# A top-k attention and expert kernel: the chain of a score tile cut from 14 steps to 12

## The chip, the cores and the metric

The kernel runs on one core of a Trainium2 chip. The metric is the device time of one execution in microseconds (us); the time of a kernel is the median of its runs, and lower is better.

## The reference

Three layers follow each other. `q`, `k` and `v` are 4 x 8 x 576 x 64 in float32, the token matrix after attention is 2304 x 512.

```python
scores = q @ k.T / sqrt(64)                       # per batch and head, 576 x 576
kth    = 32nd largest score of each row
attn   = softmax(where(scores >= kth, scores, -1e9))
x      = attn @ v                                 # 2304 x 512
h      = max(x @ w1, x @ w2, x @ w3);  x = h @ w_out      # 512 -> 768 -> 512
e      = argmax(x @ w_gate); gate = softmax weight of e     # 8 experts
out    = gate * (relu(x @ ew1[e]) @ ew2[e])       # 512 -> 1024 -> 512
```

## The kernel before, in words

**Tiles.** The scores are worked through in 144 tiles of 128 rows by 576 columns (36 for each of the 4 batches). Four tiles that follow each other make a group (`G = 4`), and some quantities, the threshold above all, are computed once for a group.

**Steps.** The order of all work is written out by hand. One loop (lines 1585 to 1735) counts steps `t`; in each step it issues, for tiles of different age, the stages below, and each engine works off its own queue in that order. A stage of tile `n` stands in step `n + L`, and the constants `L_...` (lines 612 to 618) are the ages. In the kernel before: ScalarE evicts the scores of tile `t + 1` (`st_evac`); VectorE takes the eight largest of each of six chunks (`st_chunks`, age 0) and merges them in a chain of small instructions (`st_rounds`, the step after); ScalarE marks the scores above the 24th (`st_over`, age 2); GpSimd takes those out (`st_rest`, 3); VectorE takes the next eight (`st_next8`, 4). After the fourth tile of a group VectorE finds the 32nd value of all four (`st_pick` at the end of one step, `st_kth` in the next, age `L_KTH` = 8 for the group's first tile).

**Behind the threshold.** Two tiles of each group are masked by VectorE: ScalarE takes the exponent (`st_exp`, age `L_MASK` = 9, first thing in the step) and VectorE multiplies it by the comparison with the threshold (`st_mask`, same step, at the end of VectorE's list `bulk`). The other two, for which `early(n)` is true, are masked before the exponent: ScalarE makes a mark (`st_gap`, age 7 or `L_MASK - 2`), GpSimd subtracts it from the scores (`st_drop`, a step later), and ScalarE's exponent comes in the middle of its step (age 9). Then for each tile ScalarE writes the upper 16-bit half of the result (`st_split`, age 10, last of ScalarE's big instructions in the step), GpSimd subtracts it to get the lower half (`st_split2`, 11), a DMA transposes both (`st_ptr`, 12), and TensorE multiplies with `v` (`st_av`, 14).

**What runs beside it.** The `bulk` list is worked off by `run_bulk`, and after each of its entries `micro` issues one instruction of every open chain, so that chains of small dependent VectorE instructions lie between larger ones. `st_kth` is such a chain of two instructions (lines 998 and 999), `st_rounds` one of five. `finish` issues what is left of a chain at the end of the step. The dense layers and the experts are cut into units, small batches of matmuls; `run_units` issues them behind the attention matmuls of a step, as a credit that grows by a fixed amount per step allows (1.08, later 1.4 and 1.8). Weights of the dense layers are split into halves in the first steps (`prep_w`, list `wq`): two pieces a step while `t < L_KTH - 2` = 6, then one.

**Buffers.** The exponents have `NE3` = 3 buffers, the split pairs `NPH` = 3, the score tiles `L_MASK + 2` = 11.

**Behind the last tile.** The loop goes on after step 144 until the last tiles have passed the chain; `finale` then works through the rest of the experts.

Of the kernel before, what the change touches and what calls it, by code (L numbers as in the profile page):

```python
# [19 lines left out]
def kernel(  # L20
# [61 lines left out]
    G = 4  # L82
# [12 lines left out]
    def attempt(ctx, general):  # L95
# [518 lines left out]
        L_REST = L_OVER + 1  # L614
        L_N8 = L_REST + 1
        L_KTH = L_N8 + G - 1 + 1
        L_EXP, L_MASK = L_KTH, L_KTH + 1
        L_SPLIT, L_LO, L_PTR, L_AV = L_MASK + 1, L_MASK + 2, L_MASK + 3, L_MASK + 5
        LAG = L_AV + 2
        NE3 = L_LO - L_MASK + 1  # L620

        with ExitStack() as p1:
            p_wt = p1.enter_context(ExitStack())
# [12 lines left out]
            wst, m_ps = [p_w.enter_context(tc.tile_pool(name="wst", bufs=6, side="right"))], []  # L636
# [34 lines left out]
            def after(n, fn):  # L671
                due.setdefault(clock[0] + n, []).append(fn)

            def chain(fns):
                chains.append(list(fns))
                return chains[-1]

            def micro():
                for c in list(chains):
                    if c:  # L680
                        fn = c.pop(0)
                        if fn is not None:
                            fn()
                    if not c:
                        chains.remove(c)

            def finish(c):
                while c:
                    fn = c.pop(0)
                    if fn is not None:  # L690
                        fn()
# [3 lines left out]
            def run_bulk():  # L695
                bulk.extend(tail_bulk)
                tail_bulk.clear()
                while bulk:
                    bulk.pop(0)()
                    micro()  # L700
# [46 lines left out]
            def split_tile():  # L747
                if clock[0] < 0:

                    tag = ("e", NE3) if lead_n[0] < NE3 else ("f", NFB)  # L750
                    lead_n[0] += 1
# [229 lines left out]
            def st_kth(g):  # L981
                kt = sm_p.tile([P, G], F32, tag="kth", name="kth") if general else hkth[:, g]
                kth[g] = kt
                if general:
                    m8 = sm_p.tile([P, 8], F32, tag="m8", name="m8")

                    def search(i):
                        wfall = wk_p.tile([P, S], F32, tag="f", name="f", bufs=NFB)
                        src = Ss[g * G + i]
                        for rnd in range(TOP // 8):  # L990
                            nc.vector.max(out=m8, in_=src)
                            if rnd < TOP // 8 - 1:
                                nc.vector.match_replace(out=wfall, in_to_replace=m8, in_values=src, imm_value=LOW)
                                src = wfall
                        nc.vector.tensor_copy(out=kt[:, i:i + 1], in_=m8[:, 7:8])
                    return chain([lambda i=i: search(i) for i in range(G)])
                return chain([
                    lambda: nc.vector.tensor_tensor(out=y8[g], in0=hsel[:, g % NHS], in1=y8[g], op=ALU.mult),
                    lambda: nc.vector.tensor_reduce(out=kt, in_=y8[g], axis=AX.X, op=ALU.add),
                ])  # L1000
# [19 lines left out]
                after(4, total)  # L1020


            def early(n):
                return n % G >= G - (ZN[n // G % len(ZN)])

            def st_gap(n):
                g, i = divmod(n, G)
                zz[n] = wk_p.tile([P, S], U16, tag="g", name="g", bufs=NGB)
                nc.scalar.activation(out=zz[n], in_=Ss[n], func=ACTF.Sign, scale=-1.0, bias=kth[g][:, i:i + 1])  # L1029

# [3 lines left out]
            def st_exp(n):  # L1034
                g, i = divmod(n, G)
                e = wk_p.tile([P, S], F32, tag="e", name="e", bufs=NE3)
                ee[n] = e
                nc.scalar.activation(out=e, in_=Ss.pop(n) if early(n) else Ss[n], func=ACTF.Exp, scale=ESC, bias=be[g][:, i])  # L1038

            def st_mask(n):  # L1040
                g, i = divmod(n, G)
                e = ee[n]
                nc.vector.scalar_tensor_tensor(out=e, in0=Ss.pop(n), scalar=kth[g][:, i:i + 1], in1=e,  # L1043
                                               op0=ALU.is_ge, op1=ALU.mult)

            def st_split(n):
                p = ee[n]
                ph = phl[n % NPH]
                nc.scalar.activation(out=ph[:, 0, 0:S], in_=p, func=ACTF.Copy)  # L1049
# [242 lines left out]
            def piece_ok(i):  # L1292

                if i >= KE:
                    return bool(e2) and i < KE + 2 * KD
                return bool(picked) and clock[0] > picked + 8 and clock[0] > FREE + (0 if i < KE // 2 else L_AV + 1)

            def piece(i):

                st = stage()  # L1300
                re = nc.sync.value_load(firsti[0:1, 0:1], min_val=0, max_val=NE - 1)
                if i < KE:
                    src = ew2[bass.ds(re, 1), i * P:(i + 1) * P, :]
                    hi, lo = (w2e(e, i) for e in range(2))
                else:
                    kk, f = divmod(i - KE, 2)
                    src = ew1[bass.ds(re, 1), kk * P:(kk + 1) * P, f * 512:(f + 1) * 512]
                    hi, lo = (W1e[0][:, e, kk, f * 512:(f + 1) * 512] for e in range(2))
                return split_piece(st, src, hi, lo)

            def half_piece(kk):

                f = half[0]
                st = stage()
                re = nc.sync.value_load(firsti[0:1, 0:1], min_val=0, max_val=NE - 1)
                return split_piece(st, ew1[bass.ds(re, 1), kk * P:(kk + 1) * P, f * 512:(f + 1) * 512],
                                   W1h[0][:, 0, kk], W1h[0][:, 1, kk])
# [211 lines left out]
            wq = [(prep_w, (i,)) for i in range(NPW + KF)]  # L1529
# [5 lines left out]
            def ok(n):  # L1535
                return 0 <= n < NTL
# [8 lines left out]
            with tc.manual_schedule():  # L1545
# [15 lines left out]
                pend_p, pend_w = [], []  # L1561
# [19 lines left out]
                t = -1  # L1581
# [6 lines left out]
                while second is None or not fin() or len(ranked) < NTT:  # L1588
# [8 lines left out]
                    must = []  # L1597
                    n = t - L_KTH
                    if ok(n) and n % G == 0:
                        must.append(st_kth(n // G))  # L1600
                    if ok(t - 1):
                        must.append(st_rounds(t - 1))
                    if ok(t):
# [1 line left out]
                    n = t - L_MASK  # L1605
                    if ok(n) and not early(n):
                        st_exp(n)
# [7 lines left out]
                    n = t - L_REST  # L1615
                    if ok(n):
                        st_rest(n)
                    n = t - L_LO
# [4 lines left out]
                    n = t - L_OVER  # L1623
                    if ok(t + 1):
                        st_evac(t + 1)
                    n = t - L_PTR
                    if ok(n):
                        st_ptr(n)
                    n = t - L_OVER
# [3 lines left out]
                    n = t - L_MASK  # L1633
                    if ok(n) and early(n):
                        st_exp(n)
                    n = t - L_MASK + 2
                    if ok(n) and early(n):
                        st_gap(n)
                    n = t - L_SPLIT
                    if ok(n):  # L1640
                        st_split(n)
                    n = t - L_MASK + 1
                    if ok(n) and early(n):
                        st_drop(n)
                    n = t - L_N8
# [6 lines left out]
                    pend_w = []  # L1652
                    if wq:

                        for f, a in wq[:2 if t < L_KTH - 2 else 1]:
                            wq.pop(0)
                            pend_w.append(f(*a))
                    elif not m_ps and not pend_w and t > 20:
                        p_w.close()
                        m_ps.append(p_m.enter_context(tc.tile_pool(name="mp", bufs=2, side="right")))  # L1660
                        ew.append(p_m.enter_context(tc.tile_pool(name="ew", bufs=1, side="right")))
                        W1h.append(ew[0].tile([P, 2, KD, 512], F16, name="W1h"))
                    elif piece_ok(len(eld)):
                        after(2, piece(len(eld)))
                        eld.append(t)
                    elif len(hld) < KD and half[0] is not None:
                        after(2, half_piece(len(hld)))
                        hld.append(t)
                    n = t - L_MASK
                    if ok(n) and not early(n):  # L1670
                        bulk.append(lambda n=n: st_mask(n))
                    run_bulk()
                    if general or t > NTL:
                        for _ in range(8):
                            micro()
                    for c in must:
                        finish(c)
                    n = t - L_AV
# [47 lines left out]
    with ExitStack() as first_time:  # L1726
        attempt(first_time, False)
    with tc.If(missed[0] > 0, preferred_fallthrough_block=False):
        with ExitStack() as second_time:
            attempt(second_time, True)  # L1730
# [29 lines left out]
```

## Time and profile before

| | |
|---|---|
| median of 3 runs | 933.54 us (931.37 to 938.38) |
| the profiled execution | 938.42 us, span 936.7 us |
| mean granted TensorE clock | 0.966 of full speed |

All rows of the next sections come from the one profiled execution. PE is TensorE, DVE is VectorE, ACT is ScalarE, POOL is GpSimd. The span reaches from the first to the last instruction; 1.7 us of the profiled execution lie around it. Names such as L1043 are lines of the kernel before.

### The profile page before, as it was taken

The numbers are of one execution on the slowest core, as the hardware profiler recorded it, in microseconds if no ns is written. First come the engines' busy times: TensorE is split into PE (matmuls) and PEld (weight loads), VectorE is DVE, ScalarE is ACT, GpSimd is POOL, SyncE is SP. The second block draws the span as 40 slices with busy tenths as digits, with TensorE's granted clock in tenths as the row PEclk, the third lists the DMA queues.
The fourth block names the chain that finished last, engine by engine and source line by source line (L and its number), as shares of the span: only waits on it lengthen the run. The fifth ranks groups of instructions, "written<-read, shape, count | busy, mean of one in ns | idle before, by whom it ended". The sixth has DMA issues, their size and how long they took to land. (4 is left out here: it accounts for less than half of the span.)

```text
span 936.7 us, 29138 instructions
## 1 busy us (share of the span) xinstructions
PE 746.2 (80%) x10606; PEld 576.4 (62%) x10606; DVE 762.9 (81%) x3108; ACT 706.0 (75%) x1464; POOL 607.0 (65%) x554
## 2 busy tenths in 40 slices
PE   1112368988868798988898899979999999999992
PEld 0001247667655677767677688757977755687871
DVE  5999999999999999998998999998862335567760
ACT  4768899999998898899987989998862231565660
POOL 2547798999897789788877889888972221110110
PEclk9999999999999899899989999999999999999996
DMA  9862978766997788699979888888977458698370
GB/s 223 266 213 64 208 153 157 132 143 119 194 159 168 138 158 164 122 199 178 187 135 171 169 143 170 170 172 140 180 149 126 131 159 309 160 310 228 84 194 16
DMA packets 372166, 155.94 MB, mean 166 GB/s; under 512 B 331932, under 2 KB 348320, under 8 KB 372001
## 3 DMA queue, kind: packets, MB, share of 16 engines
q1 hardware_dynamic: 368128, 143.10, 74.5%
q0 software_dynamic: 3136, 9.46, 3.0%
q8 instruction: 87, 1.43, 0.7%
q10 hardware_dynamic: 736, 1.32, 0.5%
q14 instruction: 79, 0.64, 0.2%
HBM read 76.06 MB, written 16.67 MB: 99 GB/s over the span
## 5 line engine op out<-in xcount | busy, mean ns | idle before, releaser
L355 PEld LDWEIGHTS <-W 128*128 128x128 f16 x4560 | 250.5, 100 | 23.4 <-issue 20.7
L355 PE MATMUL mm<-xT,W 128*128 128x128 f16 x3456 | 213.8, 224 | 13.4 <-DVE vl L741 5.9
L960 POOL TENSOR_TENSOR f<-s,g 128x576 f32<-128x576 f32 x144 | 189.8, 1318 | 53.2 <-ACT g L954 32.6
L1053 POOL TENSOR_TENSOR phl<-e,phl 128x576 f16<-128x576 f32 x144 | 185.8, 1290 | 7.3 <-ACT phl L1049 5.3
L908 DVE MAX8 c<-s 128x8 f32<-128x96 f32 x864 | 175.3, 243 | 9.3 <-ACT s L894 5.5
L887 PEld LDWEIGHTS <-qT 128*128 128x128 f16 (+1 forms) x640 | 56.3, 107 | 193.9 <-issue 160.6
L887 PE MATMUL S<-kt,qT 128*128 128x64 f16 (+3 forms) x320 | 61.6, 344 | 109.4 <-ACT s L894 93.9
L1072 PE MATMUL av<-vh,pt 128*128 128x65 f16 (+3 forms) x1600 | 111.7, 201 | 12.5 <-DVE xn L1121 10.3
L954 ACT ACTIVATE g<-s,bf 128x576 uint16<-128x576 f32 x144 | 111.7, 776 | 5.6
L1038 ACT ACTIVATE e<-s,be 128x576 f32<-128x576 f32 x144 | 109.7, 762 | 8.3 <-POOL phl L1053 5.4
L969 DVE MAX8 vec<-f 128x8 f32<-128x576 f32 x144 | 108.8, 756 | 4.7 <-POOL f L960 2.0
L1043 DVE SCALAR_TENSOR_TENSOR e<-s,hkth,e 128x576 f32<-128x576 f32 x72 | 103.7, 1440 | 10.6 <-ACT e L1038 7.1
L894 ACT ACTIVATE s<-S 128x576 f32<-128x576 f32 x144 | 91.8, 637 | 19.9 <-PE S L887 13.3
L1072 PEld LDWEIGHTS <-pt 128*128 128x128 f16 (+3 forms) x2400 | 90.1, 103 | 25.3 <-issue 11.5
L1049 ACT ACTIVATE phl<-e 128x576 f16<-128x576 f32 x144 | 96.3, 668 | 6.8 <-DMA pt<-phl 6.8
L1072 PE MATMUL av<-vl,pt 128*128 128x64 f16 (+3 forms) x800 | 101.0, 198 | 0.0
L1032 POOL TENSOR_TENSOR s<-s,g 128x576 f32<-128x576 f32 x72 | 97.7, 1357 | 0.3
L456 DVE SCALAR_TENSOR_TENSOR W<-st,W 128x1024 f16<-128x1024 f32 x56 | 65.8, 1221 | 38.1 <-ACT W L455 34.9
L887 PE MATMUL S<-kT,qT 128*128 128x512 f16 (+3 forms) x320 | 48.9, 293 | 23.9 <-ACT s L894 23.9
L1156 POOL TENSOR_TENSOR hhl<-a,hhl 128x384 f16<-128x384 f32 x36 | 35.9, 998 | 37.1 <-ACT hhl L1155 35.0
L455 ACT ACTIVATE W<-st 128x1024 f16<-128x1024 f32 x56 | 55.6, 1047 | 1.8 <-DMA st<-in_moe_w_dram 1.8
L1029 ACT ACTIVATE g<-s,hkth 128x576 uint16<-128x576 f32 x72 | 54.7, 760 | 0.0
(233 smaller groups left out, 1577.7 us busy)
## 6 DMA issues: line engine op xcount, KB each, us to landing
st<-in_moe_w_dram SPq DMA_DIRECT2D x72, 512.0 KB
st<-in_moe_w_dram SPq DMA_DIRECT2D x28, 256.0 KB
raw<-in_moe_w_dram SPq DMA_DIRECT2D x12, 512.0 KB
st<-in_v_dram SPq DMA_DIRECT2D x16, 256.0 KB
hs<-he SPq DMA_DIRECT2D x16, 256.0 KB
hTe<-hs SPq DMA_DIRECT2D x8, 512.0 KB
st<-in_q_dram SPq DMA_DIRECT2D x15, 256.0 KB
qT<-qT SPq DMA_DIRECT2D x30, 128.0 KB
```

What stands on the lines that cost most here:

```text
L355: nc.tensor.matmul(out=ps[:, o * n:(o + 1) * n], lhsT=w(b, kk, c), rhs=x(a, kk), start=(kk == 0 and i == 0), stop=(kk == KD - 1 and i == 2))
L887: nc.tensor.matmul(out=ps[o:o + m, j, 0:(REM if j else NQ * P)], lhsT=qt[:, vv, hh, 0:m], rhs=kr[:, hh] if j else km[:, hh // HG, :, hh % HG],
L908: nc.vector.max(out=c[:, i * 8:(i + 1) * 8], in_=s[:, i * CW:(i + 1) * CW])
L954: nc.scalar.activation(out=gg[n], in_=Ss[n], func=ACTF.Sign, bias=bf[g][:, i], accum_out=cnt[g][:, i])
L960: nc.gpsimd.tensor_tensor(out=ff[n], in0=Ss[n], in1=gg.pop(n).bitcast(F16), op=ALU.subtract)
L969: bulk.append(lambda: nc.vector.max(out=y8[g][:, i, 1:9], in_=y))
L1032: nc.gpsimd.tensor_tensor(out=Ss[n], in0=Ss[n], in1=zz.pop(n).bitcast(F16), op=ALU.subtract)
L1038: nc.scalar.activation(out=e, in_=Ss.pop(n) if early(n) else Ss[n], func=ACTF.Exp, scale=ESC, bias=be[g][:, i])
L1043: nc.vector.scalar_tensor_tensor(out=e, in0=Ss.pop(n), scalar=kth[g][:, i:i + 1], in1=e, op0=ALU.is_ge, op1=ALU.mult)
L1049: nc.scalar.activation(out=ph[:, 0, 0:S], in_=p, func=ACTF.Copy)
L1053: nc.gpsimd.tensor_tensor(out=ph[:, 1, 0:S], in0=p, in1=ph[:, 0, 0:S], op=ALU.subtract)
L1072: nc.tensor.matmul(out=av[o:o + m, i, 0:n], lhsT=t[0:kk, p * NCH + c, o:o + m], rhs=v_rows(x, b, c, hh)[:, 0:n], start=(c == 0 and p == 0 ...
```

## The change

`L_MASK` becomes 8, the age of the threshold: exponent and mask now stand in the step in which the threshold of the group's first tile is computed, and the marks of the early tiles one step sooner. `st_split` moves from the step behind the mask into the mask's own step, and from its old place to behind `run_bulk`. The lower half, the transpose and the multiplication follow at ages 9, 10 and 12 (before 11, 12 and 14). `st_gap` and `st_mask` call `finish(kth_ops[g])`, so that both instructions of `st_kth` are issued ahead of them. The exponents keep 3 buffers, the score tiles have 10. The weight pieces are split two a step until step 12, and the pool of the dense layers may open at step 20.

```diff
-        L_EXP, L_MASK = L_KTH, L_KTH + 1
-        L_SPLIT, L_LO, L_PTR, L_AV = L_MASK + 1, L_MASK + 2, L_MASK + 3, L_MASK + 5
+        L_MASK = L_KTH
+        L_SPLIT, L_LO, L_PTR, L_AV = L_MASK, L_MASK + 1, L_MASK + 2, L_MASK + 4
         LAG = L_AV + 2
-        NE3 = L_LO - L_MASK + 1
+        NE3 = 3
...
+            kth_ops = []
...
             def st_gap(n):
                 g, i = divmod(n, G)
+                finish(kth_ops[g])
...
             def st_mask(n):
                 g, i = divmod(n, G)
+                finish(kth_ops[g])
...
                     if ok(n) and n % G == 0:
-                        must.append(st_kth(n // G))
+                        kth_ops.append(st_kth(n // G))
+                        must.append(kth_ops[-1])
...
                     if ok(n) and early(n):
                         st_gap(n)
-                    n = t - L_SPLIT
-                    if ok(n):
-                        st_split(n)
...
-                        for f, a in wq[:2 if t < L_KTH - 2 else 1]:
+                        for f, a in wq[:2 if t < 12 else 1]:
...
-                    elif not m_ps and not pend_w and t > 20:
+                    elif not m_ps and not pend_w and t > 19:
...
                     run_bulk()
+                    n = t - L_SPLIT
+                    if ok(n):
+                        st_split(n)
```

## Rows read from the trace of the kernel before

**Rows 1.** The page: busy tenths of two engines in 40 equal slices of the span

```profile
PE   1112368988868798988898899979999999999992
DVE  5999999999999999998998999998862335567760
```

**Rows 2.** Windows: stretch, its length, then busy us of PE, PEld, DVE, ACT, POOL

```profile
16.60:664.70 648.10, 497.35 (x7114) 387.26 (x7114) 616.57 (x2779) 576.06 (x1264) 531.47 (x452) 0.96 0.83 164
664.70:727.00 62.30, 60.28 (x975) 51.06 (x973) 31.87 (x101) 31.84 (x65) 39.62 (x38) 1.00 0.82 144
727.00:870.00 143.00, 139.62 (x1753) 99.84 (x1751) 76.02 (x184) 63.62 (x93) 24.21 (x31) 1.00 0.75 214
```

**Rows 3.** Timeline of ACT: start, duration; the last eviction of scores (tile 143)

```profile
664.70 0.65 ACT L894 ACTIVATE s<-S 128x576 f32<-128x576 f32 x1 [1.54 <-PE S L887]
```

**Rows 4.** Timeline of PE: the first matmul of tile 143 with v

```profile
722.21 0.19 PE L1072 MATMUL av<-vh,pt 128*128 128x65 f16 x1
```

**Rows 5.** Groups of DVE instructions by line: busy us, mean ns, idle before them

```profile
L1043 DVE SCALAR_TENSOR_TENSOR e<-s,hkth,e 128x576 f32<-128x576 f32 x72 | 103.7, 1440 | 10.6 <-ACT e L1038 7.1 <-ACT phl L1049 2.9
L1150 DVE TENSOR_TENSOR a<-a,mm 128x384 f32<-128x384 f32 x72 | 39.1, 542 | 17.0 <-PE mm L355 14.1 <-ACT xhl L1093 2.2
...
L858 DVE TENSOR_SCALAR bits<-raw 128x512 int32<-128x512 int32 x24 | 16.4, 684 | 3.0 <-DMA raw<-in_moe_w_out_dram 1.9 <-DMA raw<-in_moe_w_dram 1.1
L1121 DVE TENSOR_TENSOR xn<-av,rec 128x256 f32<-128x256 f32 x36 | 14.6, 405 | 0.2
```

**Rows 6.** Timeline of DVE around the first threshold instruction (L998), in the main stretch

```profile
303.98 0.16 DVE L978 SCALAR_TENSOR_TENSOR heq<-vec,bf 128x4 f16<-128x4 f32 x1
304.06 0.41 DVE L908 MAX8 c<-s 128x8 f32<-128x96 f32 x2
304.39 0.18 DVE L998 TENSOR_TENSOR vec<-hsel,vec 128x36 f32<-128x36 f16 x1
304.48 0.20 DVE L923 MAX8 T<-c 128x8 f32<-128x48 f32 x1
```

**Rows 7.** Timeline of DVE: the last group's threshold, with nothing in between

```profile
686.86 0.16 DVE L978 SCALAR_TENSOR_TENSOR heq<-vec,bf 128x4 f16<-128x4 f32 x1
687.06 0.20 DVE L998 TENSOR_TENSOR vec<-hsel,vec 128x36 f32<-128x36 f16 x1
687.29 0.20 DVE L999 TENSOR_REDUCE hkth<-vec 128x4 f32<-128x36 f32 x1
```

**Rows 8.** Timeline of DVE: three of the 72 masks

```profile
78.61 1.78 DVE L1043 SCALAR_TENSOR_TENSOR e<-s,hkth,e 128x576 f32<-128x576 f32 x1
...
369.02 6.94 DVE L1043 SCALAR_TENSOR_TENSOR e<-s,hkth,e 128x576 f32<-128x576 f32 x1
...
681.96 1.46 DVE L1043 SCALAR_TENSOR_TENSOR e<-s,hkth,e 128x576 f32<-128x576 f32 x1
```

**Rows 9.** Timeline of ACT: the splits of the same steps, and an eviction

```profile
77.01 0.67 ACT L1049 ACTIVATE phl<-e 128x576 f16<-128x576 f32 x1
...
369.15 0.68 ACT L1049 ACTIVATE phl<-e 128x576 f16<-128x576 f32 x1
...
376.05 0.65 ACT L894 ACTIVATE s<-S 128x576 f32<-128x576 f32 x1 [5.54 <-DVE e L1043]
...
683.14 0.67 ACT L1049 ACTIVATE phl<-e 128x576 f16<-128x576 f32 x1
```

**Rows 10.** Timeline of ACT: the exponent of an early tile, then another tile's split

```profile
304.68 0.76 ACT L1038 ACTIVATE e<-s,be 128x576 f32<-128x576 f32 x1
305.34 0.67 ACT L1049 ACTIVATE phl<-e 128x576 f16<-128x576 f32 x1
```

**Rows 11.** Tile phl, who waited for it: us, times

```profile
  ACT e L1038: 5.4, 7
```

**Rows 12.** Line 1043, duration of one in ns, shortest/median/longest

```profile
L1043 DVE SCALAR_TENSOR_TENSOR e<-s,hkth,e x72: 801/1238/6940, 73.6 to 693.5; 128x576 f32<-128x576 f32 x72
```

**Rows 13.** Timeline of POOL: one of six instructions that follow each other during the longest mask

```profile
369.75 1.28 POOL L1032 TENSOR_TENSOR s<-s,g 128x576 f32<-128x576 f32 x1
```

## The prediction

> **What bounds the kernel now.** I read the page's busy tenths first, to see that there are two regimes and where they meet. VectorE is full from the second slice to about the 28th, TensorE from there to the last but one [rows 1]. The windows put numbers on it, and the reader should look at who has no idle time left in each [rows 2]. From the first eviction of scores at 16.6 us to the last at 664.7 us VectorE is busy 616.57 of 648.10 us, 95.1%; ScalarE has 89%, GpSimd 82%, TensorE 77%. From 664.7 to 870 us TensorE is busy 60.28 of 62.30 and then 139.62 of 143.00 us, while VectorE is half idle. So up to tile 143 a microsecond of VectorE work is a microsecond of time; behind it a microsecond of TensorE work is one. Third come timelines of the steps around threshold, mask and split, because the change is one of order, and only there can one see which instruction waits for which.
>
> **The drain gets two steps shorter.** Tile 143 is evicted at 664.70 us [rows 3], in step 142, and its product with v begins at 722.21 us [rows 4], in step 157: 57.5 us for 15 steps, 3.83 us a step. The change takes 2 of them out: -7.7 us. What fills these steps is TensorE work (units and products), and it doesn't vanish: the units start two steps sooner in the loop and have been done by tile 143, in the 23% of the main stretch in which TensorE is idle. If they find no room there, the term is 0; -7.7 and 0 are its ends, and I take -7.7, since the credit lets units run from the first finished block on, and that block comes two steps sooner.
>
> **Work that now lies ahead of tile 143.** Two more tiles pass mask, normalization and dense layer before the last eviction, where VectorE is the bound, instead of behind it, where it is half idle. Per tile that is (103.7 + 39.1 + 14.6)/144 = 1.09 us of VectorE [rows 5]; two tiles are 2.2 us. ScalarE and GpSimd get more too, but have 11% and 18% idle time there.
>
> **The threshold's two instructions lose their cover.** Today L998 and L999 come one by one out of the chain, between chunks. In 34 of the 36 groups the end of the step before (L978) is followed by a chunk 0.08 us after its start, and L998 by the next instruction after 0.09 us [rows 6]: they overlap. The change makes `st_gap` issue both at the start of the step, ahead of the chunks, so that L978, L998 and L999 stand in a row, and each needs what the one before wrote or read. The last group, where there are no chunks, shows what such a row costs: 0.20 us from L978 to L998, 0.23 us from L998 to L999 [rows 7]. The difference is 0.12 + 0.14 = 0.26 us for a group, and 34 groups are 8.8 us. The ends are 0 (if VectorE would have waited anyway at the start of these steps) and 8.8; I take 8.8 times VectorE's 95%.
>
> The rows show a start-to-start distance that depends on what stands between. The Trainium skill (VectorE: DVE Perf Modes, "The DRAIN you can't avoid") says that the pipeline is flushed after every VectorE instruction and that leaving out semaphores changes nothing; by that the order would be free, and the sum 8.4 us lower. The rows at 0.08 and 0.20 us differ, so the trace doesn't agree, for these small instructions.
>
> VectorE's two terms together: (2.2 + 8.8) x 0.951 = **+10.5 us**.
>
> **ScalarE's split waits for the mask of its own step.** This is the wait that is added, in two steps of four. Behind it on ScalarE stand the next step's exponent, splits of inputs and the eviction for which VectorE's chunks wait. What it costs can be read off before: in each step with a mask, compare the end of the mask [rows 8] with the start of the last split on ScalarE in that step [rows 9]. The first such step has the mask's end at 80.39 us and the split at 77.01 us: ScalarE would stand still for 3.38 us. In the last step with a wait the mask ends at 683.42, 0.28 us behind the split's start at 683.14. Of all 71 steps that can be compared 54 show no wait (the split comes later than the mask, 0.8 us in the median over all), 17 do, with 29.0 us in all. Three of these, 10.4 us, lie in the first steps, where the next eviction is 3.4 to 5.5 us ahead of its chunk. One has 6.8 us, at the mask of 6.94 us, and there the eviction at 376.05 us has waited 5.54 us for the same mask already. Against the lead of the following eviction, nearly all of the rest is covered. Ends 0 and 13.1 us (29.0 - 10.4 - 5.5); I take +1.
>
> **The early tiles: split right behind their exponent.** Exponent and split follow each other today at 0.66 us, for two different tiles; the exponent alone takes 0.76 us [rows 10]. When the split reads that exponent, it can't start before its end, and no row of ScalarE shows such a pair. Below nothing is excluded, since the same two instructions run. The other end is the 0.03 us that such a pair on VectorE leaves behind the first one's end [rows 7], so 0.79 - 0.67 = 0.12 us for 72 tiles, 8.6 us of ScalarE, which isn't the bound: I take +1.
>
> **Exponents find a free buffer.** With 3 buffers kept and the lower half one step behind the exponent instead of two, ScalarE's 5.4 us of waits for GpSimd's lower half [rows 11] go. Ends -5.4 and 0; on an engine with 11% idle I take -1.
>
> **The weight pieces** are only shifted: the same 24 pieces. Their loads have made VectorE wait 3.0 us [rows 5]; closer together they could make it wait as long again, or the freed later steps give it back: between -3 and +3, I take 0. The queue order of transposes, products and GpSimd's instructions is unchanged relative to each other, apart from the age of the tile; a mask, a mark and the first threshold instruction meet in other steps, which the totals above contain.
>
> **Sum:** -7.7 + 10.5 + 1 + 1 - 1 = **+3.8 us**, so 942.2 us against the profiled execution's 938.42. That execution lies 4.9 us above the median of the runs; put on the median, 933.54 + 3.8 = **937 us**. About 1%, 9.3 us, is what a measurement of this kernel can tell from no change.
>
> **The rivals.**
> *The row of threshold instructions is free.* VectorE stands at the step's start waiting for something else, or the flush is paid anyway: -8.4 us from the sum, 929 us. For it: a few of these steps do start with a wait for the eviction. Against it: the rows at 0.08 and 0.20 us.
>
> *The masks get shorter.* A mask takes 0.80 us at best, 1.24 in the median, 6.94 at worst [rows 12]; during that worst one six GpSimd instructions in a row ran, from before its start to 0.6 us before its end [rows 13]. If ScalarE, held at the split, feeds GpSimd later, such rows break up; all that exceeds the median, 103.7 - 72 x 1.24 = 14.6 us, times 0.951, would go: 923 us. The Trainium skill (SBUF — State Buffer, "Who interferes with whom") has the rule: a VectorE instruction with two SBUF inputs and a GpSimd instruction that reads SBUF exclude each other for a whole instruction. The trace agrees (0.80 against 6.94 us). Against the rival: the work that GpSimd does in such a row was ready before.
>
> *The split's wait is passed on: slower.* ScalarE, held back to the mask's end, evicts after VectorE has run out of chunks. It decides where the wait exceeds the eviction's lead of 0.9 us in the median. All of the 13.1 us that no cover is shown for: 3.8 - 1 + 13.1 = 15.9, so 949 us. For it: two engines at 95% and 89% that now meet twice in four steps. Against it: 54 of 71 steps without a wait.
>
> *The shorter chain isn't a shorter drain.* The units find no room sooner, and TensorE has the same work left at tile 143: the 7.7 us don't come, 945 us. Against it: 23% idle TensorE time.
>
> **How the numbers follow.** Forecast 0.50 (its own range 930 to 945, from the ends of the small terms), free row 0.17, shorter masks 0.13, passed-on wait 0.15, no shorter drain 0.05. The range leaves out the outer half of the masks' case and most of the passed-on wait: 923 to 948. Faster by over 1% (below 924.2) is the masks' case and a sliver of the free row, 0.14; slower (above 942.9) the passed-on wait, the missing drain and a tail of the forecast, 0.21; within 1% 0.65.
>
> **What would show it.** Tile 143's product should begin 13 steps and about 50 us behind its eviction; the last eviction should come some 10 us later than 664.7. L998 should follow L978 at 0.20 us and L999 at 0.23. Idle ScalarE time before the split should name the mask's line, a few us in all, and the wait for GpSimd's lower half should be gone. I am wrong if the last eviction comes earlier than today, if evictions wait for the mask step after step, or if the masks' mean leaves 1.44 us by more than 0.15.

## The result, and the profile after

The changed kernel takes 942.18 us in the median of 6 runs (940.31 to 944.47), the kernel before on the same chip 933.68: ratio **1.0088**, 95% interval 1.0060 to 1.0116. That is 8.5 us slower, a little under the 1% that the prediction called the limit of what can be told, with an interval that excludes no change. Its profiled execution took 944.47 us with a span of 942.8 us: 6.1 us more than the profiled execution of before. All rows here are from that one; in the kernel after the mask is line 1047 (before 1043), the exponent 1041 (1038), the split 1053 (1049), the product with v 1076 (1072).

The page after, busy tenths of TensorE and VectorE in 40 slices (answers to [rows 1]):

```profile
PE   1111458888878789988987998997989999999991
DVE  5999999999999989989988899997962326476760
```

Windows after, of the same three stretches (answers to [rows 2]); columns as there:

```profile
16.71:674.87 658.16, 502.72 (x7261) 398.30 (x7261) 610.53 (x2780) 584.31 (x1270) 529.01 (x454) 0.96 0.82 163
674.90:732.00 57.10, 53.59 (x798) 43.89 (x795) 28.52 (x98) 28.14 (x57) 36.55 (x35) 0.97 0.67 126
732.00:875.00 143.00, 141.74 (x1768) 100.96 (x1766) 75.42 (x186) 63.31 (x93) 25.52 (x32) 1.00 0.76 219
```

Timelines after, of ScalarE and of TensorE: the last eviction of scores, and the first product of tile 143 (answers to [rows 3, 4]):

```profile
674.87 0.65 ACT L894 ACTIVATE s<-S 128x576 f32<-128x576 f32 x1
...
727.35 0.19 PE L1076 MATMUL av<-vh,pt 128*128 128x65 f16 x1
```

Here the 6.1 us can be split. The last eviction comes 10.2 us later (664.70 to 674.87). The drain from there to the product of tile 143 is 5.0 us shorter (57.51 to 52.48 us). What follows takes 215.4 us instead of 214.5. So +10.2 - 5.0 + 0.9.

The loss lies in the stretch in which VectorE was the bound, and the windows show that it isn't VectorE's work. That fell, 616.57 to 610.53 us. Its idle time grew, from 31.5 to 47.6 us (658.16 - 610.53). The work fell because the masks got shorter; the groups of VectorE after (answer to [rows 5]), and behind it durations of one in ns, shortest/median/longest (answer to [rows 12]):

```profile
L1047 DVE SCALAR_TENSOR_TENSOR e<-s,hkth,e 128x576 f32<-128x576 f32 x72 | 87.5, 1215 | 4.7 <-ACT e L1041 4.7
```

```profile
L1047 DVE SCALAR_TENSOR_TENSOR e<-s,hkth,e x72: 797/1110/4882, 73.9 to 703.7; 128x576 f32<-128x576 f32 x72
```

103.7 us have become 87.5, a mean of 1.44 us 1.22, and the longest mask 4.88 us instead of 6.94. The idle time is in VectorE's waits between the first and the last eviction, after; columns are line, what it waited for, us in all, times, longest:

```profile
DVE hl L741 <- ACT mm L740: 18.0, 12, 4.5
DVE c L908 <- ACT s L894: 10.0, 12, 1.7
DVE e L1047 <- ACT e L1041: 3.1, 6, 1.8
```

The same waits of the kernel before, in its stretch up to the last eviction:

```profile
DVE e L1043 <- ACT e L1038: 6.1, 8, 2.2
DVE c L908 <- ACT s L894: 5.5, 8, 1.6
DVE hl L741 <- ACT mm L740: 4.5, 4, 2.4
```

L740 is ScalarE's copy of an input, L741 VectorE's subtraction that makes its lower half. With the smaller waits for L740 on other tiles VectorE stands 20.1 us there instead of 6.1, and 10.0 instead of 5.5 before its chunks. (At the weights of the last experts, `W1e`, it waits for L740 too, 10.3 us instead of 4.6, but at 759 us and later, where it isn't the bound.)

ScalarE has the new waits that the prediction spoke of. Idle time of engines before instructions on the split pairs (phl), after:

```profile
  DVE e L1047: 15.7, 11
...
  DMA pt<-phl: 13.8, 11
```

The first line is the split that waits for the mask of its own step, 15.7 us in 11 waits. The other is the split that waits until an earlier pair has been transposed; in the kernel before that was 6.8 us, 8 times, in the kernel e6_cover_pieces below, which is slower than before too, 9.2 us. Up to the last eviction alone it is 8.4, 3.4 and 3.8 us. The exponent of an early tile and its split, on ScalarE's timeline after (answer to [rows 10]), and the threshold's row on VectorE's, in the main stretch (answer to [rows 6]):

```profile
92.53 0.76 ACT L1041 ACTIVATE e<-s,be 128x576 f32<-128x576 f32 x1
93.33 0.68 ACT L1053 ACTIVATE phl<-e 128x576 f16<-128x576 f32 x1
...
224.05 0.16 DVE L978 SCALAR_TENSOR_TENSOR heq<-vec,bf 128x4 f16<-128x4 f32 x1
224.25 0.20 DVE L998 TENSOR_TENSOR vec<-hsel,vec 128x36 f32<-128x36 f16 x1
224.48 0.20 DVE L999 TENSOR_REDUCE hkth<-vec 128x4 f32<-128x36 f32 x1
224.59 0.41 DVE L908 MAX8 c<-s 128x8 f32<-128x96 f32 x2
```

### The profile page after: what moved, and what is told of

It reads as the page before. It is cut to its first block, busy times and chain, and to the rows that moved or that the text cites. A ratio compares the mean times of both kernels' runs of the same rounds, so it can differ in the third digit from the quotient of the medians.

```text
span 942.8 us, 29167 instructions
## 1 busy us (share of the span) xinstructions
PE 747.6 (79%) x10606; PEld 582.2 (62%) x10606; DVE 753.6 (80%) x3108; ACT 711.1 (75%) x1464; POOL 601.9 (64%) x554
## 5 line engine op out<-in xcount | busy, mean ns | idle before, releaser
L355 PEld LDWEIGHTS <-W 128*128 128x128 f16 x4560 | 255.4, 102 | 28.3 <-issue 25.4
L355 PE MATMUL mm<-xT,W 128*128 128x128 f16 x3456 | 222.6, 228 | 23.6 <-DVE he L1427 12.6
L1053 ACT ACTIVATE phl<-e 128x576 f16<-128x576 f32 x144 | 97.5, 677 | 31.7 <-DVE e L1047 15.7
L894 ACT ACTIVATE s<-S 128x576 f32<-128x576 f32 x144 | 91.6, 636 | 10.1 <-PE S L887 10.0
L456 DVE SCALAR_TENSOR_TENSOR W<-st,W 128x1024 f16<-128x1024 f32 x56 | 65.8, 1220 | 35.8 <-ACT W L455 35.8
L1035 POOL TENSOR_TENSOR s<-s,g 128x576 f32<-128x576 f32 x72 | 93.7, 1301 | 0.3
L1047 DVE SCALAR_TENSOR_TENSOR e<-s,hkth,e 128x576 f32<-128x576 f32 x72 | 87.5, 1215 | 4.7 <-ACT e L1041 4.7
L1154 DVE TENSOR_TENSOR a<-a,mm 128x384 f32<-128x384 f32 x72 | 39.0, 542 | 15.9 <-PE mm L355 15.2
```

Of the source, the lines that this page charges most:

```text
L355: nc.tensor.matmul(out=ps[:, o * n:(o + 1) * n], lhsT=w(b, kk, c), rhs=x(a, kk), start=(kk == 0 and i == 0), stop=(kk == KD - 1 and i == 2))
L894: nc.scalar.activation(out=s, in_=Sps.pop(n).rearrange("p a b -> p (a b)")[:, 0:S], func=ACTF.Copy, scale=DOWN)
L1035: nc.gpsimd.tensor_tensor(out=Ss[n], in0=Ss[n], in1=zz.pop(n).bitcast(F16), op=ALU.subtract)
```

## The experiments

Each kernel was timed in five rounds against the kernel before on the same chip; the median of before was 937.9, 938.2, 936.3 and 935.4 us in the four sets, so ratios are compared and not times. "Idle" is VectorE's, from the first to the last eviction of scores, "masks" the sum of the 72 masks, "drain" the time from the eviction of tile 143 to its first product; these three and the last eviction come from one profiled execution of each. Such an execution is one draw: those of before, changed and e4_split_next took 4.7, 2.3 and 7.3 us more than the median of their kernel's runs, the others lie within 3 us of theirs. Differences of a few us in these columns are therefore not firm by themselves.

| kernel | steps | ratio, 95% interval | last eviction | drain | masks | idle |
|---|---|---|---|---|---|---|
| before | 14 | 1 | 664.7 | 57.5 | 103.7 | 31.5 |
| changed | 12 | 1.0088, 1.0060 to 1.0116 | 674.9 | 52.5 | 87.5 | 47.6 |
| e1_pieces | 12 | 1.0054, 1.0030 to 1.0078 | 672.7 | 52.3 | 85.5 | 47.8 |
| e2_cover | 12 | 1.0071, 1.0045 to 1.0097 | 670.4 | 52.2 | 92.7 | 44.5 |
| e3_hoist | 14 | 1.0047, 1.0019 to 1.0074 | 669.7 | 57.5 | 102.6 | 33.8 |
| e4_split_next | 13 | 1.0036, 1.0005 to 1.0067 | 676.9 | 52.5 | 110.3 | 30.8 |
| e5_split_same | 13 | **0.9904**, 0.9871 to 0.9937 | 660.2 | 50.9 | 91.2 | 35.8 |
| e6_cover_pieces | 12 | 1.0040, 1.0016 to 1.0064 | 669.3 | 52.1 | 92.3 | 43.4 |
| e7_same_early_w | 13 | 0.9973, 0.9944 to 1.0002 | 668.0 | 51.7 | 93.3 | 40.3 |
| e8_hold | 14 | 1.0007, 0.9981 to 1.0032 | 666.0 | 56.3 | 99.0 | 36.9 |
| e9_q_sooner | 12 | 1.0046, 1.0024 to 1.0069 | 671.2 | 52.0 | 93.7 | 47.2 |
| e10_q_lead | 12 | 1.0011, 0.9986 to 1.0037 | 669.4 | 52.2 | 93.1 | 43.1 |
| e11_same_lead | 13 | 0.9936, 0.9912 to 0.9960 | 664.9 | 50.9 | 92.8 | 37.0 |
| e12_mask_sooner | 13 | 1.0023, 0.9998 to 1.0048 | 668.8 | 52.4 | 109.6 | 27.9 |

**The threshold's row, undone: e2_cover.** The changed kernel, with two pairs of chunks issued ahead of the mark, so that L998 and L999 lie between chunks again:

```diff
             def st_gap(n):
                 g, i = divmod(n, G)
+                for _ in range(2):
+                    if bulk and kth_ops[g]:
+                        bulk.pop(0)()
+                        micro()
                 finish(kth_ops[g])
```

> The changed kernel (942 us, 8.4 us over the kernel before), with one thing undone: the first two pairs of chunks are issued ahead of the mark, so that the two threshold instructions lie between chunks again, as in the kernel before. Theory A (the bare row of threshold instructions costs 0.26 us of VectorE in 34 groups): L978 to its follower back at 0.08 us, and some 8 us less, about 934. Theory B (the loss is ScalarE held at the split until the mask's end; VectorE has idle time anyway, so the row is free): unchanged within 2 us, about 942.

VectorE's timeline of this kernel, same group as above:

```profile
223.48 0.16 DVE L978 SCALAR_TENSOR_TENSOR heq<-vec,bf 128x4 f16<-128x4 f32 x1
223.56 0.41 DVE L908 MAX8 c<-s 128x8 f32<-128x96 f32 x2
223.89 0.18 DVE L998 TENSOR_TENSOR vec<-hsel,vec 128x36 f32<-128x36 f16 x1
223.98 0.20 DVE L923 MAX8 T<-c 128x8 f32<-128x48 f32 x1
```

The distances are those of before again, 0.08 and 0.09 us. The ratio goes from 1.0088 to 1.0071 only, about 1.6 us, inside both intervals; in the profiled executions the last eviction comes 4.5 us sooner.

**The row alone: e3_hoist.** The kernel before, both threshold instructions issued at the start of their step:

```diff
-                        must.append(st_kth(n // G))
+                        finish(st_kth(n // G))
```

> The kernel before, with only this part of the change: both threshold instructions are issued at the start of their step, ahead of the chunks. Chain, mask and split as before. Theory A: the main stretch is 8 us longer, about 942. Theory B: VectorE is the bound here more than in the changed kernel, but if the row is free anyway, within 2 us of 934.

1.0047: 4.4 us (1.8 to 6.9). The drain is the same, so all of it lies ahead of tile 143, whose eviction is 5.0 us late. The row exists and costs time where VectorE is full, half of what was forecast for it.

**The weight pieces: e1_pieces and e6_cover_pieces.** The changed kernel, and that of e2_cover, with two pieces a step only until step 6, as before:

```diff
-                        for f, a in wq[:2 if t < 12 else 1]:
+                        for f, a in wq[:2 if t < 6 else 1]:
```

> The changed kernel, with the weight pieces as in the kernel before (two a step until step 6, then one). In the changed kernel the eviction of tile 24 comes 4.0 us later than before (139.6 against 135.6 us), in the kernels that keep the old pieces 0 to 0.7 us later. Theory P (the pieces crowded into steps 6 to 11 cost this): tile 24 back at some 136 us, and 3 to 4 us less, about 0.5% over the kernel before. Theory Q (what comes early there is the chain itself, two tiles' masks and the held ScalarE): tile 24 stays at 138 to 140, and the time within 2 us of the changed kernel, 0.9% over before.

> 12 steps with both undone: the threshold instructions between the chunks as in e2_cover, and the old weight pieces. If the two parts (the bare row, some 4 us, and the pieces, some 4 us) are all that the 12 steps lose against the 13 steps of e5_split_same (0.990 of before), this one is at 0.99 to 1.00 of before. If exponent and mask in the threshold's step cost by themselves (masks, threshold and normalization meet in one step of four), it stays at 1.003 to 1.006.

From 1.0088 to 1.0054 and from 1.0071 to 1.0040: 0.34% and 0.31%, about 3 us in both; neither difference is clear of its intervals alone. Where it goes can be seen in the first steps. The evictions of tile 16 in before, in the changed kernel and in e1_pieces are at 104.87, 110.33 and 105.49 us. By tile 24 they are at 135.61, 139.56 and 138.15 us: the ratio is the one that theory P gave, the place of tile 24 the one that theory Q gave. With both undone the kernel is still 0.4% slower than before, with two steps fewer.

**The split alone: e5_split_same.** The kernel before, only the split moved into the mask's step behind `run_bulk`, with lower half, transpose and product one step sooner; exponents and masks stay where they were:

```diff
-        L_SPLIT, L_LO, L_PTR, L_AV = L_MASK + 1, L_MASK + 2, L_MASK + 3, L_MASK + 5
+        L_SPLIT, L_LO, L_PTR, L_AV = L_MASK, L_MASK + 1, L_MASK + 2, L_MASK + 4
         LAG = L_AV + 2
-        NE3 = L_LO - L_MASK + 1
+        NE3 = 3
...
-                    n = t - L_SPLIT
-                    if ok(n):
-                        st_split(n)
...
                     run_bulk()
+                    n = t - L_SPLIT
+                    if ok(n):
+                        st_split(n)
```

> The kernel before with only the split moved into the mask's step, behind the list (13 steps). Threshold, marks and masks where they were; the threshold's row has its cover. Theory A: one step less of drain (-2.6 to -4), the wait +1 to +4: about 933. Theory B: the held ScalarE brings most of the 8.4 us also here: 938 or more. If the split's wait is what shortens the masks, their sum falls from 103.7 to about 88 us here.

**0.9904**: 928.74 us (6 runs) against 937.88, faster than both kernels. Its window up to the last eviction, its masks, and VectorE's wait that stood out in the changed kernel:

```profile
16.04:660.19 644.15, 499.49 (x7228) 391.89 (x7228) 608.40 (x2779) 581.88 (x1267) 533.33 (x454) 0.97 0.86 166
```

```profile
L1043 DVE SCALAR_TENSOR_TENSOR e<-s,hkth,e 128x576 f32<-128x576 f32 x72 | 91.2, 1267 | 11.6 <-ACT e L1038 11.1
```

```profile
DVE hl L741 <- ACT mm L740: 11.2, 10, 2.6
```

The split waits 15.4 us for masks here too, in 11 waits, as in the changed kernel (15.7 us, 11 waits). Such waits alone therefore don't make a kernel slower. VectorE's work falls by 8.2 us against [rows 2], its idle time grows by 4.2, not by 16.

**The masks a step sooner, without the split: e4_split_next and e12_mask_sooner.** The first is the changed kernel with the split at its old place a step behind the mask; the second has the cover of e2_cover and the pieces of before as well, so it is the kernel before with marks, exponents and masks one step sooner. (Like every kernel made from the changed one it also keeps the dense layers' pool that may open at step 20 instead of 21; no run took that apart.)

```diff
-        L_SPLIT, L_LO, L_PTR, L_AV = L_MASK, L_MASK + 1, L_MASK + 2, L_MASK + 4
+        L_SPLIT, L_LO, L_PTR, L_AV = L_MASK + 1, L_MASK + 2, L_MASK + 3, L_MASK + 5
...
                     if ok(n) and early(n):
                         st_gap(n)
+                    n = t - L_SPLIT
+                    if ok(n):
+                        st_split(n)
...
                     run_bulk()
-                    n = t - L_SPLIT
-                    if ok(n):
-                        st_split(n)
```

> The changed kernel with the split in the step behind the mask again, at its old place (13 steps). Mask, exponents and the bare row of threshold instructions stay in step 8. Gone: the wait of ScalarE for the mask of its own step, and the split right behind its exponent (0.79 instead of 0.67 us). The drain is one step longer (+2.6 to 4 us). Theory A (the row is most of the loss): about 940. Theory B (the held ScalarE is most of it): about 935 or less, with ScalarE's wait for the mask's line and VectorE's waits for ScalarE's copies of inputs (17.6 us in the changed kernel, 4.5 before) back at the values of before; the masks, 87.5 us in the changed kernel, back at some 100.

> The kernel before with only the marks, exponents and masks one step sooner (in the threshold's step), the threshold's instructions between chunks and the weight pieces as before; the split stays a step behind the mask, so the chain has 13 steps. Open is why the kernel with the split in the mask's step gives 0.990 and the one with the masks a step sooner as well gives 1.004, although that has a step less. Theory M, the sooner mask costs by itself: the same 1.4% that lies between those two falls on the kernel before, so about 1.010 here, with late evictions of tiles 60 to 120. Theory I, it costs only where the split stands in the same step as well: about 0.996 to 0.999 here (one step of the drain, 3.8 us, or what the kernel with the split next gave, 1.0036, less 0.0015 for the bare row and 0.0033 for the pieces), VectorE's waits for ScalarE's copies near 13 us as in the kernel with the split next, not near 30. A ratio between 1.001 and 1.007 would leave both open.

1.0036 and 1.0023: neither gains from its shorter chain. The second lies in the band that was said to leave both theories open, and it does as far as the ratio goes. Its window and its masks tell more:

```profile
16.95:668.83 651.88, 497.09 (x7185) 390.63 (x7184) 623.99 (x2780) 577.45 (x1268) 530.59 (x454) 0.95 0.82 164
```

```profile
L1051 DVE SCALAR_TENSOR_TENSOR e<-s,hkth,e 128x576 f32<-128x576 f32 x72 | 109.6, 1522 | 9.6 <-ACT e L1045 9.3
```

```profile
DVE hl L741 <- ACT mm L740: 6.6, 7, 1.9
```

Sooner masks alone make VectorE's work 7.4 us longer (the masks 5.9 of it), and its idle time doesn't grow. With the split in the same step (e6_cover_pieces) the masks fall to 92.3 us, but the idle time is 43.4 us:

```profile
16.68:669.30 652.62, 502.22 (x7261) 395.07 (x7261) 609.23 (x2780) 584.64 (x1269) 531.41 (x454) 0.96 0.82 164
```

```profile
DVE hl L741 <- ACT mm L740: 17.6, 13, 4.0
```

**The pieces again: e7_same_early_w.** The kernel of e5_split_same with two pieces a step until step 12:

> e5_split_same (13 steps, 0.990 of before) with only the weight pieces of the change: two a step until step 12. Theory P: 3 to 4 us more, 0.994, and tile 24 evicted 3 to 4 us later than the 136.3 us there. Theory Q: the same as e5_split_same within 2 us, tile 24 at some 136 us.

From 0.9904 to 0.9973, 0.69%: crowded pieces alone take back most of that gain.

**Is it the holding of ScalarE that shortens the masks? e8_hold.** The kernel before; behind `run_bulk` ScalarE copies one column of the masked exponent, which nothing reads, and so waits for the mask as the split would:

```diff
                     run_bulk()
+                    n = t - L_MASK
+                    if ok(n) and not early(n):
+                        held = sm_p.tile([P, 1], F32, tag="held", name="held", bufs=2)
+                        nc.scalar.activation(out=held, in_=ee[n][:, 0:1], func=ACTF.Copy)
```

> The kernel before with the wait alone: behind the list, in the steps with a mask, ScalarE copies one column of the masked exponents to a spare tile, which nothing reads; the split stays a step later, the chain has 14 steps. This holds ScalarE until the mask's end without shortening anything, and adds 72 small instructions of about 0.2 us on ScalarE. Theory H (holding ScalarE keeps GpSimd from running a long row of instructions against the mask): the masks' sum falls from 103.7 to about 90 us, those over 2 us from 26.7 to 15 or less, and the last eviction of scores comes earlier than 664.7 or stays; drain 58 us as before; time 0 to 5 us under before. Rival (the masks are shorter because the lower half and the transpose come at another time in the step, not by the hold): masks stay at 100 or more, and the time is 3 us or more over before for the wait and the 72 instructions.

The masks take 99.0 us, 4.7 less than in before, where the split itself takes off 12.5 (e5_split_same). Holding ScalarE is at most a small part of it. ScalarE waited 11.3 us for masks in this kernel, in 8 waits, and the ratio of 1.0007 prices the holding, with its 72 small copies, at 0.7 us (-1.8 to 3.0). Where the masks differ can be read: those of over 2 us are 7 with 26.7 us in before, 2 with 9.3 in the changed kernel, 3 with 13.1 in e5_split_same, 7 with 23.7 here and 8 with 32.7 in e12_mask_sooner, while all others together take 75.3 to 78.2 us in these five. Why the long ones come and go stays open.

**Do the input copies come too late? e9_q_sooner, e10_q_lead, e11_same_lead.** The kernel of e6_cover_pieces with each piece of q loaded and split one step sooner; then with the load a step sooner and the split where it was; then this last edit on e5_split_same:

```diff
-                    items.append((need - 2, need - 6, prep_q, (b, qb)))
+                    items.append((need - 2, need - 7, prep_q, (b, qb)))
```

> e6_cover_pieces (12 steps, threshold covered, old weight pieces, 1.004 of before), with the blocks of q loaded and split one step sooner. In the 13 steps of e5_split_same the split of a q block falls into the step right behind the two masked steps; in 12 steps the masks have moved one step ahead and the q split has not. Theory R (that meeting is what the 12 steps lose: VectorE's waits for ScalarE's copies of q, 30.2 against 16.9 us, all in that one step of four): shifted along, they fall to 20 or less, and the time to 0.99 to 0.995 of before. Theory S (masks, threshold and normalization in one step of four cost by themselves): unchanged at 1.002 to 1.006.

> e6_cover_pieces, with the blocks of q loaded one step sooner but split in the same step as before, so that the load has two steps to land instead of one. Theory L (the load is late: ScalarE's wait for q loads, 10.2 us here against 2.6 in e5_split_same, and VectorE behind it): that wait falls to 3 us or less, the time to 0.993 or so. Theory R: the wait falls, but the time stays above 1.0, since the split still falls into the wrong step. Theory S: unchanged at 1.002 to 1.006.

> e5_split_same (13 steps, 0.990 of before), with the blocks of q loaded one step sooner and split in the same step as before. Theory L: there are 2.6 us of waits for q loads left to gain, 0.988. Theories R and S: within 0.002 of e5_split_same. It could become the fastest kernel of the study.

1.0046 and 1.0011, where the kernel without them has 1.0040; and 0.9936, where it has 0.9904. Copies that only come a step sooner change nothing; more lead for the load may give 0.3%, with intervals that overlap, and doesn't help e5_split_same. Up to the last eviction VectorE's waits for L740 fall from 19.9 us to 12.5 in e10_q_lead (before had 6.1), yet its idle time there stays, 43.4 and 43.1 us. ScalarE's waits in that stretch, of e6_cover_pieces and behind it of e10_q_lead, show that the time has moved, from the loads of q to the split that waits until an earlier pair is transposed:

```profile
ACT hl L757 <- DMA st<-in_q_dram: 10.2, 4, 4.5
...
ACT phl L1057 <- DMA pt<-phl: 3.8, 4, 1.6
```

```profile
ACT phl L1057 <- DMA pt<-phl: 13.6, 11, 2.6
...
ACT hl L757 <- DMA st<-in_q_dram: 2.6, 1, 2.6
```

No run gave the split pairs a fourth buffer, so whether that wait is the limit is untested. The 0.29% are about a fifth of the 1.36% between e6_cover_pieces and e5_split_same; with the earlier load in both, 12 and 13 steps still lie 0.75% apart.

## Why the prediction was right, and where its steps were not

The forecast was +3.8 us with a range that reaches to +14 above the median; +8.5 was measured, more than twice the forecast. The sign, the +10 us at the last eviction and the shorter drain came as written. That the sum stayed in its range is in good part luck, because mistakes of opposite sign met: the threshold's row was priced some 7 us too high, the sooner masks, the weight pieces and the drain too low. And the premise that up to tile 143 a microsecond of VectorE's work is a microsecond of time didn't hold: its work fell by 6.0 us, and that stretch became 10.1 us longer. The steps one by one:

**Drain, -7.7: measured -5.0.** The prediction divided 57.5 us by 15 steps and took two shares. The table shows that the second step gave no time: 50.9 to 52.5 us in the five kernels of 13 steps, 52.0 to 52.5 in the six of 12. Yet TensorE had less left to do. Windows of the drain, of before, of e5_split_same and of the changed kernel, columns as in [rows 2]:

```profile
664.70:722.21 57.51, 55.49 (x880) 46.37 (x877) 30.41 (x93) 31.21 (x63) 39.62 (x38) 1.00 0.89 156
```

```profile
660.19:711.04 50.85, 49.86 (x766) 40.94 (x763) 25.27 (x92) 29.36 (x61) 38.70 (x36) 1.00 0.90 161
```

```profile
674.87:727.35 52.48, 49.60 (x721) 40.12 (x718) 27.22 (x91) 27.68 (x56) 36.58 (x35) 0.97 0.73 137
```

The first count is that of the matmuls in the drain: 879 or 880 in the kernels of 14 steps, 766 to 812 with 13, 720 or 721 with 12. So the units did move ahead of tile 143, as forecast. But in all six kernels of 12 steps, and in no other, TensorE waits 2.5 us in the drain for VectorE's work on the products of a dense layer (L1154), and right behind that wait its granted clock is 0.5 for 3.4 us, 1.2 instead of 2.4 GHz. The changed kernel's timeline shows the same batch of 36 matmuls ahead of the wait and behind it:

```profile
681.89 2.17 PE L355 MATMUL mm<-xT,W 128*128 128x128 f16 x36
686.61 3.69 PE L355 MATMUL mm<-xT,W 128*128 128x128 f16 x36 [2.55 <-DVE a L1154]
```

The wait of 2.55 us and the 1.52 us that the second batch takes longer are together 4.1 us, about a step's share. No run took the wait out. The rival of no shorter drain, given 0.05, so has the second step's time on its side, but not its mechanism: the work left at tile 143 was not the same.

**VectorE's two terms, +10.5: the eviction came 10.2 us later, but for other reasons.** The distances in the threshold's row were as forecast: 0.20 us in 35 of the 36 groups (0.18 in one), and 0.23 us in all. (In before the chunk follows L978 after 0.08 us in 32 groups, not 34; in two more it comes 0.45 and 0.49 us behind.) Their time was mis-sized: 4.4 us where VectorE is full (e3_hoist), 1.3 to 1.6 in the changed kernel (1.0088 to 1.0071, 1.0054 to 1.0040), where it stands still anyway. The end 0 of that term was given for just this case, and the value was taken near the other end. That the order isn't free stands: L998 begins 0.20 us behind L978 in the row, and with a chunk between the instruction behind L978 begins after 0.08 us, in e2_cover as in before. The section that the prediction weighed against its rows (the Trainium skill, VectorE: DVE Perf Modes, "The DRAIN you can't avoid") doesn't make the order free, though the prediction read it so: it also says, "A next op that is not held starts earlier". This trace agrees with that sentence: the chunk begins 0.08 us into an instruction of 0.16 us.

**The split's wait, +1: not contradicted.** There were 15.7 us of it in 11 waits, 7.5 us of them in the first three (up to 100 us) and 8.2 behind, where the prediction had expected "a few us". e5_split_same has nearly the same waits and is faster, and e8_hold puts holding ScalarE at 0.7 us.

**Exponent and split, +1: the end that was named.** Of the 72 pairs 63 stand at 0.79 to 0.80 us, as the bound of 0.79 said; in the other nine the split waits for an earlier pair to be transposed. **Exponents' buffer, -1:** ScalarE's waits for GpSimd's lower half, 5.4 us in before [rows 11], don't occur in the trace after; their price in time wasn't measured by itself.

**Weight pieces, 0: too low.** 0.31% and 0.34%, about 3 us, the upper end of the -3 to +3; on e5_split_same 0.69%, beyond it and clear of both intervals.

**Shorter masks, a rival with 0.13: the shortening came, its gain did not.** The masks fell by 16.2 us, more than the 14.6 of the rival, and by 0.22 us in the mean, which crosses the mark of 0.15 that the prediction had set against itself. All nine kernels with the split in the mask's step have masks of 85.5 to 93.7 us, the other five 99.0 to 110.3. The rival's cause, ScalarE held at the split, is by e8_hold at most a small part of that. In e5_split_same this is a gain. In the changed kernel it turns into idle time: -6.0 us of work, +16.1 us of idle. So the loss is in kind what the passed-on wait described, VectorE standing still for ScalarE, at the copies of inputs (14.0 us more) more than at the evictions (4.5 us more), and not caused by the split's wait by itself.

**The step that failed most** is the sentence that masks, marks and threshold "meet in other steps, which the totals above contain": it priced the sooner mask at nothing. Along one path the change adds up as follows: split into the mask's step 0.9904; masks a step sooner 1.0040; bare row 1.0054; pieces 1.0088. In parts of 933.7 us that is -9.0, +12.7, +1.3 and +3.2, and the second is the largest. Along the other path the sooner masks alone give 1.0023, and the split on top of that 1.0040. So the two moves don't add: 0.9904 and 1.0023 would make 0.9927, and 1.0040 was measured, 1.1% or 10.6 us more (about 4.5 us to either side, by the three intervals). The four profiled executions alone make it 15.1 us, half as much again, so they split it only roughly. The drain would have been 50.9 + 52.4 - 57.5 = 45.8 us and is 52.1: 6.3 us, of which the wait and the lower clock shown above are some 4. The last eviction would have come at 660.2 + 668.8 - 664.7 = 664.3 us and came at 669.3: 5.0 us, in which VectorE stands still more (43.4 us of idle time where 35.8 + 27.9 - 31.5 = 32.2 would add up). Another 3.7 us lie behind tile 143's product. The first part is shown by the drains of all kernels. The second isn't firm: e11_same_lead, which differs from e5_split_same only in earlier loads, evicts tile 143 at 664.9 us, 4.7 us later. Why ScalarE's copies come late when mask and split stand in the threshold's step is **not settled**: sooner copies didn't cure it, and an earlier load only moved ScalarE's wait to the transposes.

## What to carry to other kernels

Before a chain is cut by two steps, try each step alone: here one step was worth -9 us and the other took back more than that. A step taken out of the time between the last input and the first output is worth its share only if the work that fills it really fits elsewhere and no new wait opens in what is left: here the second step did move TensorE's work, and a wait of 2.5 us with 3.4 us at half the clock took the gain back. So look at that stretch's waits and granted clock, not only at its steps. And an engine at 95% can be given less work and end later: ask who feeds it, and look at its idle time beside its busy time.

## What had not been expected of the hardware

The same 72 masks on VectorE, 128x576 with two inputs, take 85.5 to 110.3 us in all, depending on where masks and split stand in the step, though VectorE's own list around them is the same in before (103.7) and e5_split_same (91.2). The Trainium skill (SBUF — State Buffer, "Who interferes with whom") names GpSimd's instructions as what shuts such a VectorE instruction out; the traces agree so far as the masks that begin while none of GpSimd's two-input instructions runs take 0.81 us in the median in every kernel, and those that begin during one take 1.18 to 1.27 and end 0.6 us behind it. The lower half that GpSimd computes moves with the split, which would fit, but no run here varied that alone.
